# Running products in place of wide reciprocals, and an exponent word moved from PSUM to SBUF, in a fused RWKV-7 and feed-forward kernel

## The chip, the cores and the metric

The kernel runs on one core of a Trainium2 chip. The core has five engines that run side by side, each with its own queue of instructions in program order: TensorE (PE, matmuls; its weight loads are PEld), VectorE (DVE), ScalarE (ACT), GpSimd (POOL) and SyncE (SP, which here issues most of the transfers). SBUF is the working memory, PSUM holds the results of matmuls in banks of 128 x 512 words. The metric is the device time of one execution in microseconds; several executions are timed, and the median counts.

## What is computed

Two layers are fused. The first is a recurrence over 768 steps for 4 batches and 8 heads of width 40:

```python
y[:, :, t] = einsum('bhd,bhde->bhe', rt, state)
Sa = einsum('bhde,bhe->bhd', state, at)
state = state * wt[:, :, None, :] - einsum('bhd,bhe->bhde', Sa, bt) + einsum('bhd,bhe->bhde', vt, kt)
```

w lies between 0.85 and 0.95. The second layer takes the 3072 x 320 result x: `h = maximum(x @ w_in, 0)`, `out = (h * h) @ w_out`, with w_in of 320 x 2048 and w_out of 2048 x 320. The weights arrive as float64, the rest as float32.

## The kernel before

The sequence is cut into chunks of C = 128 steps: 24 chunks, in the order of `order`. Within a chunk the recurrence becomes matmuls, once the products of w from the chunk's middle (MID = 64) to each step, and their inverses, are known.

**Preparation of a chunk** is the generator `early` (L353), advanced one `yield` at a time by whoever schedules it. Step 1 transposes w into a PSUM bank of the pool ps_w (four banks; L360, by `turn`, L327). Step 2 makes running products by eight scans on DVE (L363, L364): `up` to the right of the middle, `down` to its left, for four pairs of heads (NP = 4). Step 3 makes the other halves as reciprocals, two instructions of 128 x 256 (L368, L369); in the form `apart=False`, used for the first four chunks, this step also transposes b and a. Step 4 (only `apart=True`) transposes b and a. Then come the products with b and a (L375, L376), the store of the decays, and the matmuls of `products`, copied out by ACT as N (L384 to L388).

**The solve** (L436) inverts triangular blocks of N on POOL by pairs of instructions (L459, L461). N reaches it through DRAM, and its result goes back through DRAM to be loaded as `blocks` or T; L493 transposes `blocks` on DVE, L495 to L512 join them.

**The chain** of a chunk (`chain`, L605) carries the state; its last products are L670 and L674 on DVE.

**The weights** are rounded from float64 in 26 pieces: ten of 128 x 512 words (w_in, w_third) and sixteen of 128 x 320 (w_out). `rounding` (L263) has two steps a piece. In the first, ACT turns the exponent bits of the piece before into a scale (Relu, L270) and starts the new piece (L274). In the second, DVE finishes the piece before (L278, L279) and then does three operations on the new one: exponent bits (L286), high mantissa bits (L287), a sum (L288). The exponent bits lie in `bits_bank`, one of the two PSUM banks of the pool ps_f, taken for good at L253. The other is `fill_bank`, into which `fill_in` (L255) sends matmuls whose results nobody reads. The float64 words are loaded into space that w_out and the hidden layer use later; a finished piece lets the next load start (`then`, L239).

**The order of the work** is written out by hand. The opening (L828 to L875) prepares chunks 0 to 3 and solves them. Then there is one slot a chunk. `opening_slot` (L924, slots 0 to 3) runs the chain of chunk i and readies chunk i + 1, with the preparation of chunks 4 to 8 spread by `fills` (L921) and the pieces of rounding by `pieces_in` (L882). `sorted_slot` (L982, slots 4 to 23) has a second set of matmuls as well, those of the feed-forward layer (`Ffn`, L690): `thirds` and `whole` (w_third, w_in into two banks of ps_f, Relu by ACT at L728), `square` (DVE, L735), `make_quarter` (w_out). Slots 4 to 7 prepare two chunks each (`ahead`, L879), the second late in the slot. After slot 23 the rest of the feed-forward layer follows.

Of the kernel before, what the change touches and what calls it, by code (L numbers as in the profile page):

```python
# [8 lines left out]
FP32 = mybir.dt.float32  # L9
I32 = mybir.dt.int32  # L10
U32 = mybir.dt.uint32
Alu = mybir.AluOpType
# [5 lines left out]
def kernel(  # L18
# [22 lines left out]
    nc = tc.nc  # L41
# [4 lines left out]
    C = 128  # L46
    MID = C // 2
    HC = C // 2
    NCH = S // C
    NP = H // 2  # L50
# [29 lines left out]
    ps_f = ctx.enter_context(tc.tile_pool(name="ps_f", bufs=2, space=PSUM))  # L80

    def psum(pool):
        name = "ps_" + pool.name[-1]
        return pool.tile([128, 512], FP32, tag=name, name=name)
# [4 lines left out]
    def single(name, shape):  # L89
        return const.tile(shape, FP32, tag=name, name=name)  # L90

    def new(name, shape, bufs):
        return work.tile(shape, FP32, tag=name, name=name, bufs=bufs)
# [4 lines left out]
    def later(fn, steps=2):  # L98
        line.append([steps, fn])
# [9 lines left out]
    def store(out_, in_, steps=2, queue=nc.sync):  # L109
        later(lambda: queue.dma_start(out=out_, in_=in_), steps)  # L110
# [53 lines left out]
    ones = single("ones", [128, MID])  # L164
# [80 lines left out]
    def fetch_weights(n, queue):  # L245
        raw, sources = fetches[n]
        for row, m_, src in sources:
            to = raw.bitcast(I32)[row:row + m_]
            if len(src.shape) == 3:
                to = to.rearrange("p (i c) -> p i c", i=src.shape[1])  # L250
            queue.dma_start(out=to, in_=src.bitcast(I32))

    bits_bank, fill_bank = psum(ps_f), psum(ps_f)  # L253

    def fill_in(cols):  # L255

        while cols:
            n = min(4, cols)
            nc.tensor.matmul(fill_bank[:, :n * 128], ident, ident.unsqueeze(1).to_broadcast([128, n, 128]),  # L259
                             start=True, stop=True, skip_group_check=True)  # L260
            cols -= n

    def rounding():  # L263

        now = None
        for n in range(len(pieces) + 1):
            before, now = now, None
            if before:
                bits = before[-1]
                nc.scalar.activation(bits, bits, Act.Relu, bias=lowest, scale=float(1 << 23))  # L270
            if n < len(pieces):
                dst, raw = pieces[n]
                words = raw.rearrange("p (f e) -> p f e", e=2)
                nc.scalar.activation(dst, words[:, :, 0].bitcast(U32), Act.Copy, scale=2.0 ** -32)  # L274
            yield
            if before:
                d_, hi, bits = before
                nc.vector.scalar_tensor_tensor(bits, hi, -(1 << 31), bits, Alu.bitwise_and, Alu.bitwise_or)  # L278
                nc.vector.scalar_tensor_tensor(d_, d_, 2.0 ** -20, bits.bitcast(FP32), Alu.mult, Alu.mult)  # L279
                finished[0] += 1  # L280
                for m_ in then.get(n - 1, ()):
                    later(lambda m_=m_: fetch_weights(m_, nc.sync), 1)
            if n < len(pieces):
                hi = words[:, :, 1].bitcast(I32)
                low, bits = words[:, :, 0].bitcast(I32), bits_bank[:, :dst.shape[-1]].bitcast(I32)
                nc.vector.tensor_scalar(bits, hi, 20, 0x7FF, Alu.logical_shift_right, Alu.bitwise_and)  # L286
                nc.vector.tensor_scalar(low, hi, 0xFFFFF, 0x100000, Alu.bitwise_and, Alu.bitwise_or)  # L287
                nc.vector.tensor_tensor(dst, low, dst, Alu.add)  # L288
                now = dst, hi, bits
            yield  # L290

    def as_they_are():
# [31 lines left out]
    def turn(x_):  # L324
        p_ = psum(ps_w)
        for q in range(NP):
            nc.tensor.transpose(p_[:, q * 128:(q + 1) * 128], pair(x_, q), ident)  # L327
        return quads(p_)

    def products(l_, r_):  # L330

        ps = [quads(psum(ps_w)) for _ in range(2)]
        for q in range(NP):
            for e in range(2):
                rows = slice(e * DP, e * DP + D)
                mm(ps[e][:, q], l_[rows, q, :], r_[rows, q, :], True)
        return ps
# [15 lines left out]
    def early(i, g=None, apart=False):  # L353

        x_ = early_loaded.pop(i)
        dec = decays.next() if g is None else kept_here[i]
        if g is not None:
            nc.vector.memset(dec[:, :A_, :, MID:MID + 1], 1.0)
        up, down, aT = (dec[:, n] for n in (UP, DOWN, A_))
        wT = turn(x_["w"])  # L360
        yield
        for q in range(NP):
            nc.vector.tensor_tensor_scan(up[:, q, MID + 1:C + 1], wT[:, q, MID:], ones, 1.0, Alu.mult, Alu.mult)  # L363
            nc.vector.tensor_tensor_scan(down[:, q, MID - 1::-1], wT[:, q, MID - 1::-1], ones, 1.0, Alu.mult, Alu.mult)  # L364
        yield
        if not apart:
            bT_, aT_ = turn(x_["b"]), turn(x_["a"])
        nc.vector.reciprocal(down[:, :, MID + 1:C + 1], up[:, :, MID + 1:C + 1])  # L368
        nc.vector.reciprocal(up[:, :, :MID], down[:, :, :MID])  # L369
        yield  # L370
        if apart:
            bT_, aT_ = turn(x_["b"]), turn(x_["a"])
            yield
        bT = turned("bT", 1)
        nc.vector.tensor_tensor(bT, bT_, down[:, :, 1:C + 1], Alu.mult)  # L375
        nc.vector.tensor_tensor(aT[:, :, :C], aT_, up[:, :, :C], Alu.mult)  # L376
        if g is None:
            store(kept_e[i], dec[:USED], 2 + opening[0])
        yield
        bb, c = order[i]  # L380
        t_ = new("N", [128, 2, H, HC], 1)
        for e, p_ in enumerate(products(bT, aT[:, :, :C])):
            plain, flip_ = t_[:, :, e:NP:2], t_[:, :, NP + e::2]
            nc.scalar.copy(plain, p_[:, ::2].rearrange("s h (f t) -> s f h t", f=2))  # L384
            for half in range(2):
                own_, other = (slice(n * HC, (n + 1) * HC) for n in (half, 1 - half))
                nc.scalar.copy(flip_[own_, half], p_[other, 1::2, other])
            nc.scalar.copy(flip_[:HC, 1], p_[:HC, 1::2, HC:])  # L388
        joins = lambda half, f=Q: t_[half * HC:half * HC + Q, half, :, f:]
        for half in range(2):  # L390
            for n in range(2):
                at = half * HC + n * Q
                if i < SMALL:
                    kept, to = kept_q[i, :, half, n], at + Q
                else:
                    u = unit_of[i]
                    kept, to = kept_d[u][i - units[u][0], :, half], (half + 1) * HC
                    kept = kept[:, n * Q * HC:n * Q * HC + Q * (to - at)].rearrange("h (s t) -> h s t", s=Q)
                store(kept.rearrange("h s t -> s h t"), t_[at:at + Q, half, :, n * Q:to - half * HC], 1 + opening[0], nc.scalar if g is not None and n else nc.sync)
            if i < SMALL and g is None:  # L400
                store(kept_m[i][half], joins(half, 0), 1 + opening[0])
        if g is None:
            store(kept_n[i], t_[:HC, 1], 1 + opening[0])
        else:
            g["dec"], g["N"] = dec, new("N21", [HC, H, HC], 2)
            nc.scalar.copy(g["N"], t_[:HC, 1])
            g["joins"] = spare("joins", i)
            for half in range(2):
                nc.scalar.copy(g["joins"][half * HC:half * HC + Q], joins(half))
        yield  # L410
# [382 lines left out]
    def prepare(i, g=None, apart=False, steps=0):  # L793
        gen = early(i, g, apart)
        for _ in range(steps):
            next(gen)
            yield
        if i + 1 < len(order) and i + 1 not in early_loaded:
            load_early(i + 1)
        yield from gen  # L800
# [17 lines left out]

    weights = moe_w_in.dtype != FP32
    rounded = rounding() if weights else as_they_are()  # L820

    def weights_by(n, queue):
# [3 lines left out]


    e0, e1, e2, e3 = (early(i, ready[i]) if i in ready else prepare(i) for i in range(B))  # L828
    r0, first_slot = rest(0, ready[0]), chain(0, ready[0])
    fill_in(4)  # L830
    go(e0, 3)
    go(e1)
    fill_in(4)
    go(e0)
    go(e1)
# [4 lines left out]
    x_["b"] = fetch("b", b, 0)  # L840
    go(e1)
    fill_in(3)
    go(r0, 2)
    go(e1)
# [234 lines left out]
```

## Time and profile before

| what | value |
|---|---|
| median of 4 runs | 971.18 us (966.96 to 973.06) |
| the profiled execution, its own time | 974.94 us |
| its span, first to last instruction | 973.2 us |
| mean granted TensorE clock | 0.935 |
| busy: PE, PEld | 910.4, 732.3 us |
| busy: DVE, ACT, POOL | 476.6, 284.9, 517.6 us |
| reciprocals L368, L369 (24 each) | 1.74, 1.70 us each |
| scans L363, L364 (96 each) | 0.27, 0.26 us each |

The profile is of one execution. A line "L376" is a line of the kernel. A row of waits reads: engine, tile and line of the instruction that waited, then `<-` and whom it waited for; us in total, number of times, longest. A row of the timeline reads: start in us, duration, engine, line, operation, tile written `<-` tiles read, partitions x elements, number of instructions merged, and in brackets the idle time before it with what ended it. A row of one line's statistics gives the shortest, median and longest duration in ns.

### The profile page before, as it was taken

The page shows a single profiled execution, that of the slowest core. Times are in us where ns is not written, and L with a number is a line of the kernel's source. Part 1 is how long each engine was busy: PE and PEld are TensorE (multiplying, and loading weights), DVE is VectorE, ACT ScalarE, POOL GpSimd, SP SyncE. Part 2 cuts the span into 40 slices and gives each one's busy share as a digit, 9 for nine tenths or more (in the row PEclk, how much of TensorE's full clock was granted, in tenths as well). Part 3 has the DMA queues.
Part 4 walks back from the last instruction along what each step waited for, and adds up shares of the span by engine and source line. Part 5 has one row for each costly group of instructions (what it writes and reads, how often), then busy time and mean ns, then how long its engine had stood idle before and what let it go on. Part 6 is the DMA issues. An engine that isn't in the chain of part 4 may idle for free.

```text
span 973.2 us, 22417 instructions
## 1 busy us (share of the span) xinstructions
PE 910.4 (94%) x9122; PEld 732.3 (75%) x9122; DVE 476.6 (49%) x872; ACT 284.9 (29%) x735; POOL 517.6 (53%) x993
## 2 busy tenths in 40 slices
PE   6977976978989999999999999999999999999998
PEld 4655755655868878788888888888888888887776
DVE  5526974877366556536655644733434323231111
ACT  3133532433322433323323422222222221222111
POOL 4788418055083846029999849999759860000000
PEclk8869765877999999999999999999999999999999
DMA  7979896974468797885762795524454353130000
GB/s 101 152 160 141 167 178 157 199 141 86 89 113 130 138 177 135 139 152 94 120 109 66 131 177 109 112 47 85 107 105 77 61 106 65 32 54 8 14 13 14
DMA packets 256314, 103.68 MB, mean 107 GB/s; under 512 B 237236, under 2 KB 243252, under 8 KB 255060
## 3 DMA queue, kind: packets, MB, share of 16 engines
q1 hardware_dynamic: 251892, 86.92, 50.7%
q0 software_dynamic: 3232, 15.21, 6.9%
q8 instruction: 72, 1.18, 0.6%
q10 hardware_dynamic: 1088, 0.13, 0.1%
q14 instruction: 30, 0.25, 0.1%
HBM read 69.33 MB, written 30.92 MB: 103 GB/s over the span
## 4 chain that ended last, share of the span: by engine, by line
PE 77%; DVE 8%; DMA 4%; issue 3%; SPq 3%; POOL 2%; ACT 2%; DVEq 0%; ACTq 0%; POOLq 0%
PE ps_f L87 40%; PE ps_w L87 15%; PE ps_c L87 12%; PE ps_w L327 5%; PE ps_c L644 1%; PE ps_c L571 1%; SPq L144 1%; PE ps_f L259 1%; PE ps_w L555 1%; POOL half_t L461 1%; DVE decay L368 1%; POOL half_p L459 1%; DMA w_out<-in_moe_w_in_dram 1%; SPq L110 1%; DMA kept_t<-half_t 1%
## 5 line engine op out<-in xcount | busy, mean ns | idle before, releaser
L459 POOL TENSOR_TENSOR half_p<-half_n,half_t 128x126 f32<-128x126 f32 (+44 forms) x437 | 227.5, 521 | 96.0 <-DMA half_n<-kept_q 30.8
L461 POOL TENSOR_TENSOR half_t<-half_t,half_p 128x126 f32<-128x126 f32 (+44 forms) x437 | 244.5, 560 | 34.2
L87 PE MATMUL ps_f<-w_out,hid 128*128 128x320 f32 x768 | 222.4, 441 | 0.0
L87 PEld LDWEIGHTS ps_f<-w_out,hid 128*128 128x128 f32 x768 | 143.6, 192 | 54.9 <-issue 2.3
L87 PE MATMUL ps_f<-tokens,w_in 128*128 128x256 f32 x672 | 156.7, 387 | 0.0
L87 PEld LDWEIGHTS ps_f<-tokens,w_in 128*128 128x128 f32 x672 | 126.0, 192 | 17.9 <-issue 1.0
L735 DVE TENSOR_TENSOR hid<-hid 128x512 f32<-128x512 f32 x96 | 82.1, 892 | 50.2 <-ACT hid L728 49.7
L728 ACT ACTIVATE hid<-ps_f 128x512 f32<-128x512 f32 x84 | 50.1, 597 | 85.5 <-PE ps_f L87 85.5
L431 POOL DMA_DIRECT2D half_n<-kept_q x18 | 9.4, 528 | 98.6 <-DMA kept_m<-N 52.2
L670 DVE TENSOR_TENSOR tokens<-ps_c,dec 128x512 f32<-128x512 f32 x24 | 16.6, 690 | 89.3 <-PE ps_c L87 89.3
L363 DVE TENSOR_TENSOR_SCAN decay<-ps_w,ones 128x64 f32<-128x64 f32 x88 | 23.9, 271 | 74.2 <-PE ps_w L327 73.2
L259 PE MATMUL ps_f<-ident 128*128 128x512 f32 (+2 forms) x114 | 56.8, 634 | 2.6 <-POOL ident masks.py:199 2.6
L87 PE MATMUL ps_f<-tokens,w_third 64*128 64x256 f32 x336 | 46.7, 383 | 4.6 <-DVE w_out L279 4.6
L384 ACT COPY N<-ps_w 128x256 f32<-128x256 f32 x48 | 17.7, 369 | 112.5 <-PE ps_w L87 75.7
L521 DVE TENSOR_TENSOR kvT<-ps_w,dec 128x512 f32<-128x512 f32 x24 | 16.6, 690 | 65.1 <-ACT minus_x L631 35.8
L343 DVE TENSOR_TENSOR RV<-ps_w,upper 128x512 f32<-128x512 f32 x48 | 30.9, 686 | 33.6 <-PE ps_w L87 33.3
L343 DVE TENSOR_TENSOR RX<-ps_w,upper 128x512 f32<-128x512 f32 x48 | 30.8, 683 | 33.4 <-PE ps_w L87 33.2
L87 PEld LDWEIGHTS ps_c<-xr,T 64*64 64x64 f32 x768 | 29.5, 144 | 19.4 <-issue 15.5
L87 PE MATMUL ps_w<-decay,bT 40*128 40x128 f32 x352 | 28.5, 293 | 15.4 <-DVE decay L376 14.8
L87 PEld LDWEIGHTS ps_w<-decay,bT 40*128 40x128 f32 x352 | 25.9, 200 | 20.8 <-DVE decay L376 18.0
L543 DVE TENSOR_TENSOR f<-end,dec 128x4 f32<-128x4 f32 x20 | 6.6, 328 | 69.8 <-DMA dec<-kept_e 69.8
L368 DVE RECIPROCAL decay<-decay 128x256 f32<-128x256 f32 x22 | 38.2, 1737 | 0.0
(131 smaller groups left out, 1448.1 us busy)
## 6 DMA issues: line engine op xcount, KB each, us to landing
kept_e<-decay SPq DMA_DIRECT2D x22, 633.8 KB
dec<-kept_e SPq DMA_DIRECT2D x22, 633.8 KB
hid<-in_moe_w_out_dram SPq DMA_DIRECT2D x16, 320.0 KB
in_w<-in_w_dram SPq DMA_DIRECT2D x24, 160.0 KB
in_ab<-in_b_dram SPq DMA_DIRECT2D x24, 160.0 KB
in_ab<-in_a_dram SPq DMA_DIRECT2D x24, 160.0 KB
in_k<-in_k_dram SPq DMA_DIRECT2D x24, 160.0 KB
in_r<-in_r_dram SPq DMA_DIRECT2D x24, 160.0 KB
```

The source lines that it names most:

```text
L87: nc.tensor.matmul(o, l_, r_, start=start, stop=True, skip_group_check=True)
L259: nc.tensor.matmul(fill_bank[:, :n * 128], ident, ident.unsqueeze(1).to_broadcast([128, n, 128]), start=True, stop=True, skip_group_check= ...
L327: nc.tensor.transpose(p_[:, q * 128:(q + 1) * 128], pair(x_, q), ident)
L343: nc.vector.tensor_tensor(t_, p_, over4(upper), Alu.mult)
L363: nc.vector.tensor_tensor_scan(up[:, q, MID + 1:C + 1], wT[:, q, MID:], ones, 1.0, Alu.mult, Alu.mult)
L368: nc.vector.reciprocal(down[:, :, MID + 1:C + 1], up[:, :, MID + 1:C + 1])
L384: nc.scalar.copy(plain, p_[:, ::2].rearrange("s h (f t) -> s f h t", f=2))
L459: nc.gpsimd.tensor_tensor(p_, part[:, at:at + m_].unsqueeze(1).to_broadcast([128, n, m_]), t3[:, :n, s:s + 1].to_broadcast([128, n, m_]), ...
L461: nc.gpsimd.tensor_tensor(t3[:, :n, s + 1:], t3[:, :n, s + 1:], p_, Alu.subtract)
L521: nc.vector.tensor_tensor(kT, kT_, down[:, :, 1:C + 1], Alu.mult)
L728: nc.scalar.activation(h_, p_.rearrange("p f t -> p (f t)"), Act.Relu)
L735: nc.vector.tensor_tensor(h_, h_, h_, Alu.mult)
```

## The change

The two wide reciprocals become two of 128 x 4, one at each end of the chunk: the inverse of the product over the whole left half, and of that over the whole right half. From these the other inverses follow by multiplying w back, in eight more scans that read the transposed w in its PSUM bank and start from the column of the reciprocal. They stand in step 3 of `early`, where the reciprocals stood.

In `rounding`, the exponent bits are written over the piece's low words in SBUF, after the sum has read them, and so become the last of the three operations; Relu, L278 and L279 then work on these words. `bits_bank` is gone, and `fill_in` takes a bank of ps_f at each call.

```diff
-    bits_bank, fill_bank = psum(ps_f), psum(ps_f)
-
     def fill_in(cols):
 
+        fill_bank = psum(ps_f)
         while cols:
...
             if before:
-                d_, hi, bits = before
-                nc.vector.scalar_tensor_tensor(bits, hi, -(1 << 31), bits, Alu.bitwise_and, Alu.bitwise_or)
-                nc.vector.scalar_tensor_tensor(d_, d_, 2.0 ** -20, bits.bitcast(FP32), Alu.mult, Alu.mult)
+                d_, hi, low = before
+                nc.vector.scalar_tensor_tensor(low, hi, -(1 << 31), low, Alu.bitwise_and, Alu.bitwise_or)
+                nc.vector.scalar_tensor_tensor(d_, d_, 2.0 ** -20, low.bitcast(FP32), Alu.mult, Alu.mult)
...
                 hi = words[:, :, 1].bitcast(I32)
-                low, bits = words[:, :, 0].bitcast(I32), bits_bank[:, :dst.shape[-1]].bitcast(I32)
-                nc.vector.tensor_scalar(bits, hi, 20, 0x7FF, Alu.logical_shift_right, Alu.bitwise_and)
+                low = words[:, :, 0].bitcast(I32)
                 nc.vector.tensor_scalar(low, hi, 0xFFFFF, 0x100000, Alu.bitwise_and, Alu.bitwise_or)
                 nc.vector.tensor_tensor(dst, low, dst, Alu.add)
-                now = dst, hi, bits
+                nc.vector.tensor_scalar(low, hi, 20, 0x7FF, Alu.logical_shift_right, Alu.bitwise_and)
+                now = dst, hi, low
...
-        nc.vector.reciprocal(down[:, :, MID + 1:C + 1], up[:, :, MID + 1:C + 1])
-        nc.vector.reciprocal(up[:, :, :MID], down[:, :, :MID])
+        nc.vector.reciprocal(up[:, :, 0], down[:, :, 0])
+        nc.vector.reciprocal(down[:, :, C], up[:, :, C])
+        for q in range(NP):
+            nc.vector.tensor_tensor_scan(up[:, q, 1:MID], wT[:, q, :MID - 1], ones[:, 1:], up[:, q, 0:1], Alu.mult, Alu.mult)
+            nc.vector.tensor_tensor_scan(down[:, q, C - 1:MID:-1], wT[:, q, C - 1:MID:-1], ones[:, 1:], down[:, q, C:C + 1], Alu.mult, Alu.mult)
```

## The prediction

> **What bounds the kernel now.** I read the page first: busy shares and the 40 slices, each 24.3 us long. The rows are PE (TensorE), DVE (VectorE) and the granted TensorE clock.
>
> ```profile
> PE   6977976978989999999999999999999999999998
> DVE  5526974877366556536655644733434323231111
> PEclk8869765877999999999999999999999999999999
> ```
>
> From the eleventh slice on PE is full at full clock; only the first ten, some 240 us, have holes. The table of stretches gives busy us of PE, PEld, DVE, ACT and POOL, then clock, DMA share and GB/s.
>
> ```profile
> 157.00:235.00 78.00, 63.19 (x656) 48.07 (x657) 64.15 (x142) 30.68 (x84) 37.85 (x100) 0.74 0.80 163
> 235.00:400.00 165.00, 158.98 (x1762) 133.33 (x1761) 88.09 (x172) 56.11 (x157) 77.39 (x204) 0.96 0.70 125
> 400.00:973.00 573.00, 569.55 (x5673) 464.70 (x5672) 231.48 (x384) 147.82 (x365) 308.48 (x400) 1.00 0.44 82
> ```
>
> After 400 us PE idles 3.5 us of 573 and the change touches no matmul that counts there: nothing to win. Between 235 and 400 it idles 6.0 us. The list of waits of PE says for whom: first for 135 to 240 us, then for 240 to 405 us (total, times, longest).
>
> ```profile
> PE ps_w L87 <- DMA spares<-kept_m: 9.0, 1, 9.0
> PE ps_w L87 <- DVE decay L376: 7.2, 1, 7.2
> PE ps_f L87 <- DVE w_out L279: 4.6, 1, 4.6
> ```
> ```profile
> PE ps_w L87 <- DVE decay L376: 6.0, 4, 2.5
> ```
>
> So every idle microsecond of 235 to 400 is PE waiting for a decay product (L376), behind the reciprocals; and the 4.6 us is PE waiting for the last rounding (L279).
>
> **Part 1, the reciprocals.** The timeline of DVE at the end of slot 7, then PE's matmul that waits for it:
>
> ```profile
> 387.33 0.26 DVE L364 TENSOR_TENSOR_SCAN decay<-ps_w,ones 128x64 f32<-128x64 f32 x1
> 387.52 1.73 DVE L368 RECIPROCAL decay<-decay 128x256 f32<-128x256 f32 x1
> 389.16 1.70 DVE L369 RECIPROCAL decay<-decay 128x256 f32<-128x256 f32 x1
> 390.77 0.63 DVE L375 TENSOR_TENSOR bT<-ps_w,decay 128x512 f32<-128x512 f32 x1
> ```
> ```profile
> 392.05 1.16 PE L87 MATMUL ps_w<-decay,bT 40*128 40x128 f32 x16 [1.17 <-DVE decay L376]
> ```
>
> Removed: two reciprocals, from 387.52 to 390.77, 3.25 us of DVE in each of 24 chunks. Added: two reciprocals of 128x4 and eight scans of 63 elements. The scans L363/L364 last 0.26 to 0.27 us but start 0.18 us apart (387.33 to 387.52), so eight take 1.45 plus 0.1 until the last is out. A reciprocal of 4 columns has no row; from below 4/256 of 1.73 us is 0.03, from above the 0.33 us that the small product L543 (128x4) takes on average, often beside POOL. I take 0.15, what L543 takes at 186.06 and 503.83 us (0.16, 0.14), and 0.05 twice for waits on a result just made (dependent pairs such as L278, L279 have a gap of 0.03). Sum 0.30 + 0.10 + 1.55 = 1.95, saving 1.3 a chunk. The dear end: the new scans start from a column that the instruction before made; if each runs alone, 0.27 + 0.03, eight take 2.4 and the saving is 0.4. The cheap end is 1.6 (free small reciprocals). I take 1.3, because the row is the same operation with the same PSUM source.
>
> Where it counts: the four waits are 2.51 (276.34 us) and three of 1.17 (315.92, 353.84, 392.05). DVE runs unbroken from L670 there to L376, so PE gains 1.3 + 3 x 1.17 = 4.8 us. What is late next in the last three is PE itself. From slot 8 on, and for the first chunk prepared in slots 4 to 7, DVE has idle time ahead of its products: worth nothing. If PE's cover were gone, it would be 1.3 a chunk.
>
> In the opening: chunk 0's scans start at 5.57 and its products end at 11.6 with DVE the only holder, so the first solve on POOL (25.0 us) comes 1.3 earlier, and with it the waits of PE at 59.8 and 93.0 us, which end when solved blocks land. At 130.2 PE waits 5.70 for L493, which stands behind two reciprocals (126.44 to 129.71): 1.3 more. But at 157.1 PE waits 9.0 us for a transfer, in a stretch with the DMA engines 0.86 busy and SP's queue issuing without a pause; of the 0 to 2.6 us won before I keep 1.3.
>
> The scans that moved still read the transposed w in PSUM, so its bank (one of four in ps_w) is held one step longer. Behind it on PE stand the transposes of b and a. In slot 4 they ran at 270.64 to 271.68, before the old scans were out at 271.89, so they do not take that bank; I price this at 0 (at most, the 1.5 us of eight scans in each of four slot ends, which would undo part 1).
>
> **Part 2, the exponent word in SBUF.** A piece on DVE in the old order, starts 0.4 to 0.5 us apart:
>
> ```profile
> 204.90 0.49 DVE L278 SCALAR_TENSOR_TENSOR ps_f<-hid,ps_f 128x320 int32<-128x320 int32 x1
> 205.43 0.49 DVE L279 SCALAR_TENSOR_TENSOR w_out<-w_out,ps_f 128x320 f32<-128x320 f32 x1
> 205.95 0.49 DVE L286 TENSOR_SCALAR ps_f<-hid 128x320 int32<-128x320 int32 x1
> 206.35 0.33 DVE L287 TENSOR_SCALAR hid<-hid 128x320 int32<-128x320 int32 x1
> 206.72 0.49 DVE L288 TENSOR_TENSOR w_out<-hid,w_out 128x320 f32<-128x320 int32 x1
> ```
>
> L287 (SBUF to SBUF) does in 0.33 what L286 (SBUF to PSUM) does in 0.49; the shift becomes an L287: 0.17 less, and 0.27 less in the ten pieces of 512 (0.69 against 0.42). But it now stands last, so the Relu on ACT (L270, 0.50 or 0.65) starts 0.6 to 0.85 later, and DVE's next piece waits for it. Eight of the 25 gaps between pieces hold nothing else (103.9, 140.6, 176.9, 182.7, 204.9, 210.9, 222.0, 231.6): there DVE loses 0.65 and wins 0.2; in the others it wins. On the sum, 17 x 0.2 against 8 x 0.45: nothing.
>
> Against it stands POOL. L735, a product of two SBUF operands, shows its range:
>
> ```profile
> L735 DVE TENSOR_TENSOR hid<-hid x96: 681/693/1744, 254.4 to 957.7; 128x512 f32<-128x512 f32 x96
> ```
>
> It takes 0.68 beside an idle POOL and up to 1.74 beside POOL's long solves; L288 likewise grows from 0.49 to 0.63 during the shorter solve of 205 to 233 us. Three more operations a piece become of that sort. The Trainium skill says why ("SBUF — State Buffer", "Who interferes with whom"): a DVE instruction with two SBUF inputs, or in a two-port mode, and a GpSimd one that reads SBUF exclude each other for a whole instruction. By that rule alone an operation could wait out a whole POOL instruction of 0.43 us, 1.3 a piece.
>
> The rows of L288 give 0.0 to 0.15 for an operation; with three more, I take 0.3 a piece beside POOL (bounds 0 and 0.45). On PE's path: at 183.3 PE waits for ACT's L638, queued behind a Relu, which comes 0.6 later: 0.5 lost. Before L376 of 213.9, four pieces (two of them close pairs, two beside POOL) cost 2 x 0.45 + 2 x 0.3 - 2 x 0.2 = 1.1 and the reciprocals at 199.5 give 1.3: 0.2 won. Bounds of this part in the opening: -5 (every close pair and every shared operation on the path) to +2 (none).
>
> **Part 3, the bank.** PE's timeline at the first matmuls of the second stage:
>
> ```profile
> 227.39 0.59 PE L87 MATMUL ps_f<-tokens,w_third 64*128 64x256 f32 x2
> 232.62 2.07 PE L87 MATMUL ps_f<-tokens,w_third 64*128 64x256 f32 x6 [4.63 <-DVE w_out L279]
> ```
>
> The first product goes to the filling matmuls' bank and runs at 227.39; the second needs the bank with the exponent words, read last by L279 of the last piece. With no such bank it follows at once: 4.6 us. What is late next: the matmuls after it use w_in, rounded by 131, tokens and ACT's copies of 224.4; the rounding of w_out ends some 20 us before its first use; DVE's next duty (L521, 248.54) had been idle 11.2 us for PE. So the 4.6 stays. A fresh bank for each filling call adds no reader and so no wait.
>
> **Sum.** Opening 1.3 - 0.5 + 0.2 = 1.0; bank 4.6; slots 4.8: 10.4 us. The profiled execution took 974.94 (span 973.2, 1.7 around it): 964.5. It lies 3.8 above the median of the four runs, 971.18, so the same gain from the median gives 960.8.
>
> **Rivals.** (a) The scans run one by one: 0.4 a chunk, slots 1.6, opening 0.4 - 0.5 - 0.7, bank 4.6: 5.4 won, 965.8. For: each has a new start operand; against: the pace of the old scans. (b) The Relu waits return: close pairs and POOL take 5 us on the path to 214 us: 10.4 - 5 - 0.7 = 4.7, 966.5. For: ACT waits 31 us for L286 already, in 14 waits; against: few of them had PE behind them. (c) The bank's wait is replaced by another: 10.4 - 4.6 = 5.8, 965.4. (d) Slower: every piece sends its Relu late, and the copies queued behind it on ACT hold PE each time: 10 x 0.85 + 16 x 0.6 = 18.1 against about 10.9 of gain without the 0.5 counted above, 978.4. It decides once some 15 of the 26 pieces delay PE; PE's waits for ACT in 60 to 240 us come to only 6 us, which speaks against it. That the reciprocals are not shortened at all would need scans dearer than any row.
>
> **Numbers.** Forecast 0.62; (a) 0.13, (b) 0.14, (c) 0.05, (d) 0.06. The forecast's own bounds: at best opening 2.6 + 2, bank 4.6, slots 1.6 + 3 x 1.17 = 5.1, so 14.3 won, 956.9; at worst opening 1.3 - 5, 5.7 won, 965.5. The range, 955 to 969, adds 2 below for the spread of the runs (6 us for four) and above takes in (a), (c) and (b) with the same spread. A measurement here separates 0.5%, 4.9 us, from no change, so faster means below 966.3: 0.75; same 0.18; slower 0.07.
>
> **What would show it.** Scans about 0.18 us apart and PE's waits for L376 after 240 us down from 6.0 to about 1.2: part 1. No wait for L279 near 227 us, the first w_third matmuls in one piece: part 3. ACT's waits for the exponent word above 31 us, and the two combining operations of a piece longer beside POOL: part 2. I would be wrong if PE waited for the w bank in the transposes of b and a, or if the opening ended later although its reciprocals are gone.

## The result, and the profile after

The changed kernel takes 966.93 us (median of 43 runs, 961.6 to 971.85), the kernel before 971.2 us in the same sessions (67 runs). The ratio is 0.9952, 95% interval 0.994 to 0.9963: 4.6 us faster, where 10.4 were forecast. The predicted range of 955 to 969 us holds the time; the forecast of 960.8 lies 6.1 us below it, and rivals (a) and (b), at 965.8 and 966.5, came closer. The profiled execution of the changed kernel took 965.89 us (span 964.2), 1.0 below its median, while that of before lay 3.7 above its own. So the two profiles differ by 9.05 us where the medians differ by 4.3: a difference between the two traces is not yet a gain, and below I take from them only what a wait or a duration shows.

Two kinds of line have moved. The changed kernel's lines are 1 or 2 lower up to the scans and 2 higher behind them: L269 is the Relu, L277 and L278 combine, L285 to L287 are the three operations on the new piece with the exponent word last, L362 and L363 the old scans, L367 and L368 the small reciprocals, L370 and L371 the new scans, L377 and L378 the decay products, L640 ACT's copy into xr.

PE's row of the page's 40 slices, then the stretch of the slots from the table of stretches (columns as in the prediction):

```profile
PE   6978875878999998999999999999999999999998
```
```profile
235.00:400.00 165.00, 159.19 (x1802) 133.93 (x1801) 84.50 (x244) 56.88 (x159) 77.57 (x204) 0.98 0.73 130
```

The picture is the one of before: the first ten slices have holes, the rest is full; after 400 us PE idles 3.5 us in both. From 157 to 235 us PE is busy 66.33 us at a clock of 0.81 (63.19 at 0.74 before). But between 235 and 400 us it still idles 5.8 us, against 6.0: the slots, where 4.8 us were to be won, kept nearly all their idle time. The waits of PE say why, first for 240 to 405 us, then for 60 to 240 us, where the second row is that of the kernel before:

```profile
PE ps_w L87 <- DVE decay L378: 3.1, 4, 1.8
PE ps_w L87 <- DVE RX L342: 2.7, 1, 2.7
```
```profile
PE ps_c L87 <- ACT xr L640: 6.9, 5, 2.1
PE ps_c L87 <- ACT xr L638: 2.2, 4, 1.1
```

The waits for the decay products fell from 6.0 to 3.1, not to 1.2, and a wait of 2.7 that before did not have stands beside them: for RX, one of the masked products that DVE copies out of PSUM. In the opening the 4.6 us for the rounding's bank (L279 of before) is gone from the list, but PE's wait for ACT's copy into xr, 2.2 us in 4 waits before, is 6.9 in 5. The end of one slot on DVE shows the new pace, the one that answers to the timeline at 387 us of before:

```profile
262.31 0.26 DVE L363 TENSOR_TENSOR_SCAN decay<-ps_w,ones 128x64 f32<-128x64 f32 x1
...
262.70 0.15 DVE L368 RECIPROCAL decay<-decay 128x4 f32<-128x4 f32 x1
262.82 0.35 DVE L370 TENSOR_TENSOR_SCAN decay<-ps_w,decay,ones 128x63 f32<-128x63 f32 x1
263.08 0.32 DVE L371 TENSOR_TENSOR_SCAN decay<-ps_w,decay,ones 128x63 f32<-128x63 f32 x1
...
264.95 0.69 DVE L377 TENSOR_TENSOR bT<-ps_w,decay 128x512 f32<-128x512 f32 x1
```

The reciprocals cost what was forecast; the scans start 0.24 us apart, not 0.18. From the start of the last old scan to the product with b it is 2.64 us (262.31 to 264.95) against 3.44 before (387.33 to 390.77), a saving of 0.8 a chunk. At the second stage's first matmuls, PE's timeline:

```profile
222.03 1.03 PE L87 MATMUL ps_f<-tokens,w_third 64*128 64x256 f32 x8
...
229.37 0.96 PE L87 MATMUL ps_c<-xr,T 64*64 64x40 f32 x16 [2.06 <-ACT xr L640]
```

All eight w_third products run at once, as forecast. Seven microseconds later, after the first sixteen w_in products, PE stands again, for ACT.

### The profile page after: what moved, and what is told of

The parts are those of the page before. It is cut to its first block, busy times and chain, and to the rows that moved or that the text cites. A ratio compares the mean times of both kernels' runs of the same rounds, so it can differ in the third digit from the quotient of the medians.

```text
span 964.2 us, 22595 instructions
## 1 busy us (share of the span) xinstructions
PE 902.9 (94%) x9122; PEld 726.8 (75%) x9122; DVE 450.7 (47%) x1064; ACT 286.4 (30%) x735; POOL 525.3 (54%) x993
## 4 chain that ended last, share of the span: by engine, by line
PE 76%; DVE 7%; DMA 5%; issue 3%; POOL 3%; SPq 3%; ACT 3%; DVEq 0%; ACTq 0%; POOLq 0%
PE ps_f L87 39%; PE ps_w L87 14%; PE ps_c L87 12%; PE ps_w L326 5%; DMA blocks<-kept_t 2%; PE ps_c L646 1%; PE ps_c L573 1%; POOL half_t L463 1%; POOL half_p L461 1%; PE ps_f L258 1%; SPq L144 1%; SPq L110 1%; PE ps_w L557 1%; DMA kept_q<-N 1%; DMA kept_t<-half_t 1%
## 5 line engine op out<-in xcount | busy, mean ns | idle before, releaser
L461 POOL TENSOR_TENSOR half_p<-half_n,half_t 128x126 f32<-128x126 f32 (+44 forms) x437 | 232.0, 531 | 97.3 <-DMA half_n<-kept_q 31.0
L463 POOL TENSOR_TENSOR half_t<-half_t,half_p 128x126 f32<-128x126 f32 (+44 forms) x437 | 247.7, 567 | 34.2
L87 PE MATMUL ps_f<-w_out,hid 128*128 128x320 f32 x768 | 219.1, 436 | 0.0
L362 DVE TENSOR_TENSOR_SCAN decay<-ps_w,ones 128x64 f32<-128x64 f32 x88 | 23.9, 271 | 69.0 <-PE ps_w L326 68.9
L87 PE MATMUL ps_w<-decay,bT 40*128 40x128 f32 x352 | 29.2, 300 | 13.1 <-DVE decay L378 10.0
L87 PE MATMUL ps_c<-xr,T 64*64 64x40 f32 x768 | 34.9, 235 | 6.9 <-ACT xr L640 6.9
L87 PEld LDWEIGHTS ps_w<-decay,bT 40*128 40x128 f32 x352 | 26.4, 206 | 18.8 <-DVE decay L378 13.4
```

The source lines that it names most:

```text
L87: nc.tensor.matmul(o, l_, r_, start=start, stop=True, skip_group_check=True)
L461: nc.gpsimd.tensor_tensor(p_, part[:, at:at + m_].unsqueeze(1).to_broadcast([128, n, m_]), t3[:, :n, s:s + 1].to_broadcast([128, n, m_]), ...
L463: nc.gpsimd.tensor_tensor(t3[:, :n, s + 1:], t3[:, :n, s + 1:], p_, Alu.subtract)
```

## The experiments

My theory after the result: the exponent word made last sends ACT's Relu late, and xr's copy, which stands behind the Relu in ACT's order, with it (**late word**). The rivals: POOL slows the rounding's operations now that they read SBUF alone (**contention**); the bank was never worth 4.6 us (**bank**); the scans are the whole shortfall (**scans**). Gains in us are differences from the kernel before on the same chip, worked out from the ratio. The ratio is not the quotient of the two medians; from the medians the gains come out up to 1.3 us different. Runs 1 to 4 are from one chip, 5 to 12 from another.

**1. The changed kernel again**, without an edit, as the measure for the next three runs.

> The changed kernel once more, as the yardstick on this chip. All theories: 4 to 5 us below the kernel before. Its profile should again show the new scans 0.24 us apart and PE waiting for ACT's L640 longer than the 2.3 us of before.

965.65 us, ratio 0.9949 (0.9928 to 0.9971), 5.0 us won. PE's waits for xr are 7.2 us here, for the decay products 3.1: the trace's two findings repeat.

**2. The scans alone.** The kernel before, with this part of the change:

```diff
-        nc.vector.reciprocal(down[:, :, MID + 1:C + 1], up[:, :, MID + 1:C + 1])
-        nc.vector.reciprocal(up[:, :, :MID], down[:, :, :MID])
+        nc.vector.reciprocal(up[:, :, 0], down[:, :, 0])
+        nc.vector.reciprocal(down[:, :, C], up[:, :, C])
+        for q in range(NP):
...
```

> Part 1 alone. Theory A (the scans cost 0.24 us each, so a chunk wins 0.75 us and not 1.3): the four slot ends win 2.9 us, the opening about 1, so 3 to 4 us below before. Rival B (the loss is all in the rounding, the scans are worth what was forecast): 6 us below before.

968.16 us, 0.9969 (0.995 to 0.9987): 3.0 us won, of 6.1 forecast for this part. The decay waits are 3.1, the bank's wait is still there with 4.2 us, xr waits are 2.2 as before.

**3. The rounding alone.** The changed kernel's `rounding` and `fill_in`, with the wide reciprocals.

```diff
-        nc.vector.reciprocal(up[:, :, 0], down[:, :, 0])
-        nc.vector.reciprocal(down[:, :, C], up[:, :, C])
...
+        nc.vector.reciprocal(down[:, :, MID + 1:C + 1], up[:, :, MID + 1:C + 1])
+        nc.vector.reciprocal(up[:, :, :MID], down[:, :, :MID])
```

> Parts 2 and 3 alone, with the wide reciprocals. Theory C (the word written last delays the Relu and the copies behind it on ACT, which eats most of the bank's 4.6 us): 0 to 2 us below before. Rival (the bank's wait is won in full and the order costs nothing): 4 to 5 us below before.

971.56 us, 0.9996 (0.9971 to 1.0021): nothing won, of 4.3 forecast for parts 2 and 3. The bank's wait is gone, and PE waits longer for xr:

```profile
PE ps_c L87 <- ACT xr L637: 10.3, 5, 5.2
```

So of a shortfall of some 6 us, part 1 alone misses 3.1 (run 2) and the rounding alone 3.9 (run 3).

**4. The word made first, in SBUF.** The changed kernel, but the exponent word has a space of its own (`bits_space`, the last 512 columns of the space of the later hidden layer, which no arriving piece takes) and is the first of the three operations again. Scans, SBUF operands and a fresh fill bank stay.

```diff
+    bits_space = free_words[:, -512:]
...
-                low = words[:, :, 0].bitcast(I32)
+                low, bits = words[:, :, 0].bitcast(I32), bits_space[:, :dst.shape[-1]].bitcast(I32)
+                nc.vector.tensor_scalar(bits, hi, 20, 0x7FF, Alu.logical_shift_right, Alu.bitwise_and)
                 nc.vector.tensor_scalar(low, hi, 0xFFFFF, 0x100000, Alu.bitwise_and, Alu.bitwise_or)
                 nc.vector.tensor_tensor(dst, low, dst, Alu.add)
-                nc.vector.tensor_scalar(low, hi, 20, 0x7FF, Alu.logical_shift_right, Alu.bitwise_and)
-                now = dst, hi, low
+                now = dst, hi, bits
```

> The changed kernel, but the exponent word goes to a space of its own in SBUF and is made first again, before the other two operations; no bank is held. Theory C (the order costs): 3 us or more below the changed kernel, some 8 us below before, and the waits of PE for L640 back to about 2 us. Rival D (operands in SBUF beside POOL cost, whatever the order): as the changed kernel within 1 us.

963.15 us, 0.9917 (0.9885 to 0.995): 8.1 us won. The same place in both kernels, first the changed one (DVE, then ACT; PE's line at 229.37 is above):

```profile
226.45 0.56 DVE L278 SCALAR_TENSOR_TENSOR w_out<-w_out,hid 128x320 f32<-128x320 f32 x1
...
228.05 0.34 DVE L287 TENSOR_SCALAR hid<-hid 128x320 int32<-128x320 int32 x1
229.04 0.49 DVE L277 SCALAR_TENSOR_TENSOR hid<-hid 128x320 int32<-128x320 int32 x1 [0.65 <-ACT hid L269]
```
```profile
228.43 0.58 ACT L269 ACTIVATE hid<-hid,lowest 128x320 int32<-128x320 int32 x1 [2.71 <-DVE hid L287]
229.03 0.60 ACT L640 COPY xr<-ps_c 64x160 f32<-64x160 f32 x2
```

The Relu starts as L287 ends, and the copy to xr that PE needs starts as the Relu ends. Now with the word first, where it is L287 of that kernel:

```profile
223.57 0.57 DVE L280 SCALAR_TENSOR_TENSOR w_out<-w_out,hid 128x320 f32<-128x320 f32 x1
224.18 0.37 DVE L287 TENSOR_SCALAR hid<-hid 128x320 int32<-128x320 int32 x1
...
225.53 0.65 DVE L279 SCALAR_TENSOR_TENSOR hid<-hid 128x320 int32<-128x320 int32 x1
```
```profile
224.58 0.56 ACT L271 ACTIVATE hid<-hid,lowest 128x320 int32<-128x320 int32 x1 [2.91 <-DVE hid L287]
225.17 0.60 ACT L642 COPY xr<-ps_c 64x160 f32<-64x160 f32 x2
```

From the combining operation's start to xr's copy it is 2.58 us with the word last (226.45 to 229.03) and 1.60 with it first (223.57 to 225.17); the other two operations run under the Relu, and DVE has no gap of 0.65. PE's waits for xr are 3.1 us in this execution. This speaks for late word; contention is the same in both kernels, which read the same kinds of operand. The Relu that runs here in a space of its own takes 0.56 us in the median, over the piece's low words (every other word) 0.59, and the combining operations take the same (0.492 and 0.494), so hardly anything of this is the place of the word.

**5. The order alone, in the PSUM bank.** The kernel before, with the exponent word made last and nothing else:

```diff
-                nc.vector.tensor_scalar(bits, hi, 20, 0x7FF, Alu.logical_shift_right, Alu.bitwise_and)
                 nc.vector.tensor_scalar(low, hi, 0xFFFFF, 0x100000, Alu.bitwise_and, Alu.bitwise_or)
                 nc.vector.tensor_tensor(dst, low, dst, Alu.add)
+                nc.vector.tensor_scalar(bits, hi, 20, 0x7FF, Alu.logical_shift_right, Alu.bitwise_and)
```

> The kernel before with one thing changed: the exponent word, still in its PSUM bank, is made after the other two operations. Theory C (the order costs): 2 to 5 us slower than before, PE's waits for ACT's L638 up from 2.2 to 7 us or more. Rival D (operands in SBUF beside POOL cost, not the order): no change.

973.06 us, 1.0016 (1.0003 to 1.0029): 1.6 us lost, with no new SBUF operand anywhere. The sign is that of late word; the size is below the 2 to 5 us that I expected, and far below the difference between runs 3 and 6. Why the order costs so little while the bank is held, no run shows. xr waits are 4.6 us, where 7 or more were expected, the bank's wait is 5.5 in place of 4.6, and ACT's waits for the word rise from 31.1 to 38.8.

**6. The word first, with the wide reciprocals.** Run 4's rounding in the kernel before.

> The kernel before, wide reciprocals and old order, with the exponent word in a space of its own in SBUF and no bank held. Theory C: the bank's wait of 4.6 us is won with little given back, 4 to 5 us below before. Rival D: 1 us or less below before.

963.53 us, 0.9914 (0.989 to 0.9938): 8.3 us won without a single scan changed, more than the 4 to 5 that I expected. Against run 3, whose only difference is where the word is made and when, it is 8.0 us; the intervals lie far apart. The decay waits are 6.0, as before, and those for xr:

```profile
PE ps_c L87 <- ACT xr L639: 2.7, 4, 1.0
```

Contention falls here as the cause: this kernel's combining operations read SBUF alone as well. So does "scans" as the whole shortfall, since runs 3 and 6 have none of the new ones.

**7. The bank taken back.** Run 4's kernel, but the last piece's exponent word goes to a PSUM bank that is held, and the fills have the other one, as in the kernel before:

```diff
+    bits_bank, fill_bank = psum(ps_f), psum(ps_f)
...
-                low, bits = words[:, :, 0].bitcast(I32), bits_space[:, :dst.shape[-1]].bitcast(I32)
+                low, bits = words[:, :, 0].bitcast(I32), (bits_bank if n == len(pieces) - 1 else bits_space)[:, :dst.shape[-1]].bitcast(I32)
```

> The version with the word made first in SBUF and with the new scans, but the last of the 26 pieces puts its word into a PSUM bank that is held for it as before, so the first matmuls of the second stage wait for that piece again. If the bank is worth what was forecast: 4 to 5 us above the version without it, so some 3 us below before, with a wait of PE for the last rounding of 4 to 5 us. Rival (a bank's wait that goes is taken by the next one): 2 us or less above it, 6 us below before.

968.08 us, 0.9959 (0.9943 to 0.9976), 4.1 us worse than run 4 by the ratios (4.6 by the gains of the medians); the two intervals overlap by a hair (0.995 against 0.9943), those with run 12 just don't. PE's list has the wait again, and xr with 2.1 us only:

```profile
PE ps_f L87 <- DVE w_out L280: 6.6, 1, 6.6
```

So freeing the bank is worth about what part 3 said, in kernels with scans, and the rival "bank" is unlikely: a worth near nothing lies at the edge of these intervals. What this wait costs besides its length is shown below.

**8. Scans from a constant.** The changed kernel with 1.0 as the start of the eight new scans; the scaling by the reciprocal is left out, so the inverse decays lack a factor.

```diff
-            nc.vector.tensor_tensor_scan(up[:, q, 1:MID], wT[:, q, :MID - 1], ones[:, 1:], up[:, q, 0:1], Alu.mult, Alu.mult)
+            nc.vector.tensor_tensor_scan(up[:, q, 1:MID], wT[:, q, :MID - 1], ones[:, 1:], 1.0, Alu.mult, Alu.mult)
...
```

> The changed kernel with the eight new scans started from the constant 1 in place of the reciprocal's column (the scaling of those inverses is left out; the two small reciprocals stay). Theory A (the start operand read from SBUF is what makes a scan take 0.24 us in place of 0.18): starts 0.18 us apart, duration 0.27. Rival (63 elements at an odd address, or PSUM read beside PE): still 0.24 apart.

DVE's timeline at two of the new scans, and PE's wait for the decay products from 240 to 405 us:

```profile
266.64 0.26 DVE L370 TENSOR_TENSOR_SCAN decay<-ps_w,ones 128x63 f32<-128x63 f32 x1
266.82 0.26 DVE L371 TENSOR_TENSOR_SCAN decay<-ps_w,ones 128x63 f32<-128x63 f32 x1
```
```profile
PE ps_w L87 <- DVE decay L378: 1.2, 1, 1.2
```

The pace is 0.18 us and the decay waits are 1.2, the numbers of the prediction. A start value that is a column in SBUF costs 0.06 us a scan, 0.5 a chunk. One execution, 966.13 us, does not measure what that is worth in time. And PE's wait for RX, 2.4 us here, remains, so it is no matter of the scans' pace.

**9 to 12. The four combinations on one chip**, since the scans and the order had not added up: wide reciprocals or scans, word last or first.

> Wide reciprocals, word made last (rounding_only once more), beside the three others of this call on one chip. If order and scans add up, by their means so far: 0.5 us below before. If the order is worth more with the wide reciprocals than with the scans: 7 us above wide_first_2.

> The changed kernel beside the three others: 5 us below before by all theories, 2 to 3 us above scans_first_2.

> Wide reciprocals, word made first in SBUF. If order and scans add up: 3 us above scans_first_2, that is 5 us below before. If the scans are worth nothing once the word is made first: level with scans_first_2, 8 us below before.

> Scans, word made first in SBUF: 8 us below before, the fastest of the four if order and scans add up.

| kernel | us | ratio to before (95%) | PE's waits for xr, here and in the first run |
|---|---|---|---|
| wide, word last | 971.42 | 1.0 (0.9978 to 1.0022) | 6.9, 10.3 |
| scans, word last (the change) | 966.7 | 0.9964 (0.9944 to 0.9983) | 5.9, 7.2 |
| wide, word first | 962.81 | 0.9913 (0.9888 to 0.9939) | 2.2, 2.7 |
| scans, word first | 963.2 | 0.9909 (0.9875 to 0.9942) | 2.9, 3.1 |

With the word last the scans bring 3.5 us here (4.6 between runs 1 and 3); with the word first, 0.4 here and none between runs 4 and 6. The order costs 5.3 us with scans (3.1 between runs 1 and 4) and 8.4 with wide reciprocals (8.0). The best kernels are the two with the word first in SBUF, at 0.991 of before, some 4 us below the change as made.

One place shows how the two parts meet, in run 3: DVE's second wide reciprocal, then ACT's Relu of the piece behind it.

```profile
94.76 1.69 DVE L368 RECIPROCAL decay<-decay 128x256 f32<-128x256 f32 x1
```
```profile
99.92 0.75 ACT L269 ACTIVATE w_out<-w_out,lowest 128x512 int32<-128x512 int32 x1 [4.65 <-DVE w_out L287]
```

A whole piece stands behind the wide reciprocals, the Relu behind its last operation, the copy into xr (101.26) behind the Relu and the next piece's start, and PE waits 5.23 us for that copy (101.60). Shorter reciprocals and an earlier word attack the same wait, so either can win part of what the other would have won: in run 6, with the word first, PE waits 0.93 us for this copy. But run 9, the same kernel as run 3, waits only 1.86 there, and most of such a wait is covered later, as the place of the order's cost shows below.

**The stretch behind the bank**, from all these traces: the time from the start of the first eight w_third products to the end of the second group of sixteen w_in products, with the same matmuls between them in every kernel, and PE's idle time in it.

| kernel | stretch, us | of it PE idle | the rest |
|---|---|---|---|
| word in the bank: before, runs 2, 5, 7 | 19.8, 18.2, 20.3, 22.1 | 4.6, 4.2, 5.5, 6.6 | 15.2, 14.0, 14.8, 15.5 |
| the change: after, runs 1, 10 | 15.8, 17.5, 17.6 | 2.7, 3.2, 3.1 | 13.1, 14.4, 14.5 |
| wide, word last: runs 3, 9 | 13.4, 15.8 | 1.9, 2.6 | 11.5, 13.1 |
| scans, word first: runs 4, 12 | 14.7, 14.6 | 1.6, 1.5 | 13.1, 13.2 |
| wide, word first: runs 6, 11 | 11.9, 12.1 | 0.6, 0.6 | 11.3, 11.4 |

The rest differs although the work is the same. The columns behind the busy times say why: the granted clock (first of the last three). The kernel before, in and behind the wait:

```profile
229.00:235.00 6.00, 2.38 (x14) 1.55 (x15) 5.83 (x11) 0.50 (x1) 4.41 (x14) 0.60 1.01 131
235.00:242.00 7.00, 7.00 (x42) 5.53 (x41) 2.34 (x3) 2.22 (x6) 0.00 (x0) 0.61 0.11 40
```

Run 6 and run 4, at the second w_third and w_in products:

```profile
227.00:234.00 7.00, 6.36 (x43) 5.22 (x40) 5.31 (x7) 3.14 (x8) 4.02 (x13) 1.00 0.34 60
```
```profile
226.00:234.00 8.00, 7.36 (x40) 5.65 (x39) 4.37 (x15) 2.70 (x7) 4.17 (x13) 0.79 0.62 93
```

Behind the bank's wait the clock is 0.6, and sixteen w_in products take 6.10 us where they take 3.72 at full clock. A finer window shows what 0.6 is made of, in the kernel before:

```profile
231.00:240.00 9.00, 7.38 (x32) 5.63 (x33) 6.27 (x9) 2.36 (x6) 2.80 (x9) 0.50 0.57 85
```

In steps of 1 us it is 0.62 from 230 on, 0.50 from 231 to 240, 0.76 up to 241, and 1.00 on both sides: half clock for 10.2 us, from 230.2 to 240.5, 7.9 of them after PE's restart at 232.62. Half of 7.9 is 3.9 us of lost work, and the rest of 15.2 us is 3.9 longer than that of run 6 at full clock, 11.3. So the wait of 4.6 us cost 8.5 us of the stretch, nearly twice its length. How much of that reaches the end is less sure: run 7's stretch is 7.4 us longer than run 4's, and its time only 4.1 by the ratios.

The stretch of runs 6 and 11 is 7.9 and 7.7 us shorter than that of before, and by the ratios these kernels are 8.3 and 8.4 us faster. That the two agree is not a full account: both executions also begin the stretch some 6 us earlier than the profiled one of before, which is 3.7 above its median, and give back 5.6 and 1.5 us behind it.

**Where the order's cost lies.** Near 155 us PE stands for 9 to 11 us in every kernel, until a transfer or DVE's product with b is there. The next column is the time from PE's restart there to the end of the stretch; the last one is the part of it in which DVE, behind the scans or reciprocals of one chunk, works off four pieces up to that chunk's product with b, for which PE waits.

| kernel | PE's restart, at us | to the end of the stretch, us | four pieces on DVE, us |
|---|---|---|---|
| scans, word last: after, runs 1, 10 | 154.3, 154.3, 155.0 | 83.6, 85.1, 85.2 | 11.4, 11.6, 11.8 |
| wide, word last: runs 3, 9 | 155.4, 157.3 | 84.0, 85.2 | 11.7, 11.7 |
| scans, word first: runs 4, 12 | 154.3, 155.7 | 79.7, 79.9 | 10.1, 10.0 |
| wide, word first: runs 6, 11 | 154.0, 154.2 | 79.2, 78.8 | 10.0, 10.0 |

The changed kernel had waited 3.0 us for xr ahead of the restart, run 4 only 1.2, and both restart at 154.3: those waits were covered. Behind it the order costs 4 to 6 us. Of these 1.4 to 1.8 are DVE's own, for the most part from two gaps of 0.65 us in the four pieces. The start of DVE's second piece there, in the changed kernel and then in run 4:

```profile
199.43 0.50 DVE L277 SCALAR_TENSOR_TENSOR hid<-hid 128x320 int32<-128x320 int32 x1 [0.66 <-ACT hid L269]
```
```profile
197.74 0.48 DVE L279 SCALAR_TENSOR_TENSOR hid<-hid 128x320 int32<-128x320 int32 x1
```

In the kernel before, with the word first in PSUM, the four pieces take 10.6 us: part of run 6's gain over it is the cheaper shift, and not the bank.

The rest of the order's cost is PE's wait for xr near 180 us (1.8 to 2.2 us with the word last, 0.95 with it first) and the stretch (13.4 to 17.6 us against 11.9 to 14.7). No run moved xr's copy ahead of the Relu, so how much goes through ACT's queue alone is read from these waits and was not tested by itself.

## Where the prediction was right and where it failed

**The step that failed most: part 2, its "0.5 lost" for one late copy on PE's path.** The "0.2 won" of the same part held: from the chunk's first scan to its product with b, with the reciprocals and the four pieces between them, it is 15.2 to 15.5 us in the changed kernel and 15.3 before, so the gaps in close pairs were priced about right. But on PE's path the prediction saw one late copy, at 183.3 us, where PE's wait grew from 1.1 to 1.8 us. What it should have followed is ACT's queue: the Relu holds every copy behind it, xr's first of all, in all pieces that stand ahead of one, also where DVE itself has no gap. In the changed kernel PE waits for xr at 102, 138, 179 and 229 us, 1.3 to 2.1 each, and the last of these, 2.1 us in the stretch where the bank's wait had just been won, has a lowered clock behind it. PE's waits for xr are 2.2 to 3.1 us in the four executions with the word first in SBUF and 5.9 to 10.3 in the six with it last in SBUF (run 8's 6.4 among them), though those ahead of 155 us are mostly covered. Against the word first, DVE's gaps included, the order costs 3 to 5 us with scans, 8 with wide reciprocals (runs 1, 3, 4, 6, 9 to 12). It was rival (b), "The Relu waits return", priced at 5 + 0.7 and given 0.14. The argument against it, that few of ACT's waits had PE behind them, was read from a kernel in which the word came early; a later word changes which of them have. That the measured 966.93 lies so near this rival's 966.5 is in part luck: neither the clock behind the bank's wait, which wins, nor the wait for RX, which loses, is in its sum.

**Part 3: the mechanism was right, the size off both ways.** The bank's wait of 4.6 us goes, and in the kernels with the word first the matmuls behind it run faster too: 12 to 15 us for the stretch in place of 18 to 22. "So the 4.6 stays" missed that second half, since I priced matmuls at the durations they had. It also failed as stated: in the change the word made last puts a wait for xr of 2.1 to 2.5 us into the same stretch, beside one of 0.6 for hid that every kernel without the held bank has, with a lowered clock behind them (0.81 from 229 to 238 us), so that it takes 15.8 to 17.6.

**Part 1: the mechanism was right, its sizes were off.** The term "1.55 (eight scans)" is 1.9 to 2.0, because the pace is 0.24, so 1.3 a chunk is 0.8, and the slot ends give 2.9 (6.0 to 3.1) in place of 4.8. Run 8 shows the start column in SBUF as the cause; rival (a) had the right suspicion, but the scans don't run one by one. Second, "What is late next in the last three is PE itself" failed: PE is earlier and meets a transfer. The new wait for RX, 2.7 us at 364.76, is DVE standing before the transposes of `blocks`, with RX (364.05) behind them in its order:

```profile
363.68 0.45 DVE L495 STREAM_TRANSPOSE spares<-blocks 128x256 f32<-128x256 f32 x1 [3.76 <-DMA blocks<-kept_t]
```

All eight executions with scans have it, with 0.7 to 2.7 us (run 2 1.0, run 8 2.4); of the six with wide reciprocals only run 6 does, with 1.3. In the changed kernel's executions it takes 1.3 to 2.7 of the 2.9 back. In run 2, 2.9 less 1.0 and the opening's forecast 1.3 make 3.2, and the scans alone won 3.0. Third, I priced the w bank held longer at nothing: in the opening PE waits 1.2 us for a ps_w bank until the new scans are done (L371, at 97.23; 1.4 in run 1, 0.8 in run 4). I had looked for this in the transposes of b and a; the matmul that waits is the product of rT and kvT.

**Contention** between DVE and POOL was priced at 0.3 us a piece beside POOL. It exists, and it is not the cause. L278 at 128 x 320, now with SBUF operands alone, takes 0.491 at best, 0.494 in the median and 0.637 at worst; run 4's L280 takes 0.491, 0.493 and 0.628, and its kernel is the fastest. The Trainium skill ("SBUF — State Buffer", "Who interferes with whom") would let one operation wait out a whole POOL instruction; the median of this row lies at its shortest, and the worst is 0.15 us above it.

**What stays open.** Why the scans bring nothing once the word is first. The two kernels differ in the stretch: 14.6 to 14.7 us with scans, 11.9 to 12.1 without. With scans PE waits 0.8 to 0.9 us for xr in it (at 227 us in run 12), without them it does not, and the clock behind is 0.79 to 0.81 in place of 1.00: 3.4 us at half clock, 1.7 lost. That is 2.6 us, about what the scans win elsewhere, in two executions of each; no run took this wait away from the kernel with scans. Nor is the difference itself sure: by the intervals of runs 4, 6, 11 and 12 a gain or a loss of some 3 us could still be there.

## What to carry to other kernels

When an operation is moved to the end of its group, don't count the group's engine alone: find who waits for its result, and then everything that stands in that waiter's queue behind the wait, with its own customers. Here the shift itself became cheaper, but ACT's queue turned a Relu that came 1 us late into PE's time. Not each such wait counts: one ahead of a longer wait for something else is covered. And when a buffer is freed, ask whether that needs the reordering that comes with it: the bank could be freed with the old order kept, and that version won nearly twice as much as the change. A wait of PE is priced with the clock that the matmuls behind it get, not by its length alone.

## What the runs showed of the hardware

- A scan of 63 elements on 128 partitions whose start value is a column in SBUF starts 0.24 us after the one before it and takes 0.32; from a constant it is 0.18 and 0.26 (run 8). Scans that don't depend on one another overlap by 0.08 us in both cases.
- A reciprocal of 128 x 256 takes 1.70 to 1.74 us, one of 128 x 4 takes 0.15 to 0.18.
- The clock behind a wait. Behind 4.2 to 6.6 us of PE's idle time (the bank) the next sixteen w_in products took 4.95 to 6.44 us, in all four kernels; at full clock they take 3.72. The Trainium skill says that a TensorE idle for a window of about 3.4 us falls to half clock until it has been busy for as long ("TensorE: Matmul & The Clock Gate", "Part 1: The HAM clock gate (the "warmup" mystery)"). The traces agree with the half and with the step: worked out from the granted clock around this stretch, half clock lasts 10.2, 6.7, 10.2 and 13.7 us (before, runs 2, 5, 7), 3.4, 6.8 and 6.7 us in the change (after, runs 1, 10), 3.4 in runs 4, 9 and 12, and there is none in runs 3, 6 and 11. All of these are near multiples of 3.4. But at the bank's wait half clock began 1.6 to 2.9 us after PE had stopped and held for 5.5 to 8.5 us after its restart, so neither keeps to a whole window of idle or of busy time. And two shorter waits, together 1.5 to 1.6 us, were followed by half clock in both kernels with scans and the word first, while 1.9 us in run 3 were not, nor 0.6 in runs 6 and 11. What decides there no run shows.
- The executions of one kernel differ by up to 10 us (961.6 to 971.85 for the changed one), so of effects of 3 us only medians of many runs and single waits in the trace tell, not two profiles side by side.
